# Attention scores as two key tiles with the mask inside the bias, and an order planned with other durations

## The chip, the cores and the metric

The kernel runs on one core of a Trainium2 chip. A core has five engines that run side by side and wait for each other by semaphores: PE (TensorE, the matrix products), DVE (VectorE), ACT (ScalarE), POOL (GpSimd) and SP, which here only issues transfers. PE writes its products to PSUM; DVE and ACT read and write PSUM and SBUF, and POOL works on SBUF. The metric is the device time of one execution in microseconds (us), lower is better.

## The reference

The program is sliding-window attention followed by a mixture of experts, all in float32.

```python
def _attn_ref(q, k, v):                 # q, k, v: (4, 8, 576, 64)
    scores = scale * np.matmul(q, k.transpose(0, 1, 3, 2))
    rel = pos[:, None] - pos[None, :]
    bias = slopes[:, None, None] * (-np.abs(rel).astype(np.float32))[None, :, :]
    mask = (rel >= 0) & (rel < window)  # window = 128
    scores = np.where(mask, scores + bias[None], -1000000000.0)
    scores = scores - np.max(scores, axis=-1, keepdims=True)
    attn = np.exp(scores)
    attn = attn / (np.sum(attn, axis=-1, keepdims=True) + 1e-09)
    return np.matmul(attn, v)

def _moe_ref(x, domain_probs, w1, w2):  # x: (2304, 512), w1: (4, 512, 1024), w2: (4, 1024, 512)
    p = domain_probs / (domain_probs.sum(-1, keepdims=True) + 1e-09)
    for e in range(E):
        h = np.maximum(x @ w1[e], 0.0)
        out += p[:, e:e + 1] * (h @ w2[e])
```

The rows of `x` are the tokens of the attention's output, with the eight heads side by side.

## The kernel before

**The experts.** The 2304 tokens are cut into seven blocks (`BLOCKS`): three of 256 tokens and four of 384. The weights come in 16 units of two tiles of hidden features each, and a pass over the units serves one, two or three blocks, so that 60 loads of both weight matrices are made in all. For one unit and one block, `hidden` makes 24 matmuls (L761) of 256 or 384 columns and `output` makes 6 matmuls of 512 columns for each 128 tokens (L823). A float32 product is made of three: each operand is split into a high part, rounded to the type fp32r that PE takes (`cast`, L278 on ACT, L280 on DVE), and a low part, the difference (`minus`, L288, on DVE or POOL). The products used are high by high, high by low, low by high. Names ending in h and l, such as w1h and w1l, xh and xl, are those parts; rh and rl are the parts of the hidden features (L782 on ACT, L789 on DVE). The output of a unit is weighted and added on DVE (L840).

**The attention.** It works on pairs of heads. A *segment* is one block and one pair of heads; a *unit* is one tile of 128 queries of a segment. There are 18 tiles times 4 pairs, 72 units. The 8 units of the first block are "plain" (PE takes their float32 operands as they are); the other 64 split queries and keys. A query sees at most 128 keys: some of its own tile, the others of the tile before. `pk` is the number of keys of the tile before: 128, or 64 or 0 near the start of a sequence, since sequences of 576 tokens start in a tile's middle. For one unit:

1. scores (L446, plain L437): for each head, queries by `pk + 128` keys, into one PSUM bank `b`.
2. fold: the window has 128 keys, so each query's scores fit in 128 columns of the SBUF tile `s`. A copy (L278 or L280) brings the columns of the tile before; `copy_predicated` on DVE (L482) overwrites with the scores of the query's own tile where a triangular mask says so.
3. `least` (L492, DVE, one for each head): bias plus negated scores, and their minimum. The profile calls it CUSTOM_DVE_ANT_0. It reads `s` and `bias`, both in SBUF; where `pk` is 0 it reads PSUM.
4. `exponents` (L504, ACT, one for each head) with their sums; two small DVE operations on two columns (L520, L529); `weights_`, the division by the sum (L536 on DVE, or L544 twice on ACT).
5. transposes on PE (L569, one for each head, 128 columns), then the high and low part (`hl`; L278/L280, L288).
6. `own` and `others` (L586, L599): POOL's affine_select parts the folded columns again into the keys of the own tile and of the tile before, in `pt`, one of three buffers.
7. values by probabilities (L635) into PSUM `av`, later summed (L658, L661) and split into xh and xl.

**The order.** Nothing is emitted as it is written. Every operation is noted with what it reads and writes, an assumed time for each engine that may take it, and a due time; `Plan.order` simulates the engines greedily, and picks engine, buffer and order from that. Operations are then emitted in the order of their simulated starts, and every engine runs its own queue strictly in that order. The assumed times are the functions `act`, `dve`, `dve2`, `pool`, `mm` at L180 to L185 and constants in `unit`, such as 0.205 us for `least`. DVE and POOL are simulated as independent. Attention of later blocks is spread between the experts' work of earlier ones.

## Time and profile before

| | before |
|---|---|
| median of 3 runs (lowest to highest) | 980.52 us (980.38 to 980.91) |
| span of the profiled execution | 977.4 us |
| median less span | 3.1 us |
| PE busy, matmuls | 925.4 us (95%), 5222 |
| DVE busy | 754.0 us (77%) |
| ACT busy | 352.2 us (36%) |
| POOL busy | 285.6 us (29%) |
| first expert matmul starts | 28.16 us |
| mean granted TensorE clock | 0.995 |

The span runs from the first to the last instruction of one profiled execution. A matmul's recorded duration contains a part in which the next one already streams, so a busy PE may still issue late; the distance between two starts tells what a matmul costs in a stream. For the other engines the busy time includes time in which an instruction has been started and is held up.

### The profile page before, as it was taken

How to read it: one execution, taken by the hardware profiler on the slowest of the kernel's cores; microseconds unless marked ns; L12 is line 12 of the kernel's file. 1: busy time of each engine (PE TensorE's matmuls, PEld its weight loads, DVE VectorE, ACT ScalarE, POOL GpSimd, SP SyncE). 2: the span in 40 equal slices, each digit the busy share in tenths (PEclk: the TensorE clock that was granted, in tenths of full speed). 3: DMA queues.
4: the chain of work that ended last, by engine and by line, in shares of the span. 5: the costliest groups of instructions: out<-in, count | busy, mean ns of one | idle time of the engine just before them, and what ended most of it. 6: DMA issues, size and time to landing. Idle time of an engine off the chain costs nothing.

```text
span 977.4 us, 14432 instructions
## 1 busy us (share of the span) xinstructions
PE 925.4 (95%) x5222; PEld 829.9 (85%) x5222; DVE 754.0 (77%) x1575; ACT 352.2 (36%) x909; POOL 285.6 (29%) x278
## 2 busy tenths in 40 slices
PE   6788898999999999999999999999999999999998
PEld 4677787888888888988888889899999999999997
DVE  5999998898889899888797787866656565656554
ACT  4655445344454555333233432343221212121210
POOL 4667543334434255322232232222101010101000
PEclk9899999999999999999999999999999999999999
DMA  9655433232333345422222211111321121211101
GB/s 235 195 173 171 143 135 114 92 105 84 106 128 117 123 144 191 138 92 83 74 92 82 74 65 58 52 44 65 103 91 66 51 76 46 67 63 65 44 1 65
DMA packets 38359, 95.67 MB, mean 98 GB/s; under 512 B 3728, under 2 KB 15888, under 8 KB 38288
## 3 DMA queue, kind: packets, MB, share of 16 engines
q1 hardware_dynamic: 38288, 94.75, 29.3%
q8 instruction: 41, 0.67, 0.3%
q14 instruction: 30, 0.25, 0.1%
HBM read 90.02 MB, written 4.72 MB: 97 GB/s over the span
## 4 chain that ended last, share of the span: by engine, by line
PE 67%; DVE 26%; issue 3%; DMA 2%; ACT 1%; POOL 1%; DVEq 0%; ACTq 0%; POOLq 0%; SPq 0%
PE b L761 31%; PE b L823 30%; DVE s L492 5%; DVE acc L840 3%; DVE w2l L288 3%; PE av L635 2%; DVE w1l L288 2%; PE b L569 2%; DVE rl L789 2%; DVE qs L288 2%; PE b L446 2%; DVE s L536 1%; DVE s L482 1%; DMA k<-in_qk 1%; DVE x L661 1%
## 5 line engine op out<-in xcount | busy, mean ns | idle before, releaser
L761 PE MATMUL b<-xh,w1h 128*128 128x384 f32 (+1 forms) x896 | 286.8, 320 | 0.0
L761 PE MATMUL b<-xl,w1h 128*128 128x384 f32 (+1 forms) x896 | 281.7, 314 | 0.2 <-DVE xl L288 0.2
L761 PE MATMUL b<-xh,w1l 128*128 128x384 f32 (+1 forms) x896 | 281.7, 314 | 0.0
L840 DVE SCALAR_TENSOR_TENSOR acc<-b,prob,acc 128x512 f32<-128x512 f32 (+1 forms) x271 | 201.7, 745 | 64.9 <-PE b L823 64.2
L782 ACT ACTIVATE rh<-b 128x384 fp32r<-128x384 f32 (+1 forms) x224 | 98.9, 442 | 402.8 <-PE b L761 400.4
L823 PE MATMUL b<-w2l,rh 128*128 128x512 f32 x578 | 227.4, 394 | 0.0
L823 PE MATMUL b<-w2h,rl 128*128 128x512 f32 x578 | 226.9, 393 | 0.0
L823 PE MATMUL b<-w2h,rh 128*128 128x512 f32 x578 | 226.4, 392 | 0.0
L789 DVE SCALAR_TENSOR_TENSOR rl<-b,rh 128x384 fp32r<-128x384 f32 (+1 forms) x224 | 111.0, 495 | 103.8 <-ACT rh L782 102.7
L761 PEld LDWEIGHTS b<-xl,w1h 128*128 128x128 f32 x896 | 170.6, 190 | 5.8 <-DVE xl L288 0.4
L761 PEld LDWEIGHTS b<-xh,w1h 128*128 128x128 f32 x896 | 170.8, 191 | 5.3
L288 POOL TENSOR_TENSOR w1l<-w1r,w1h 128x512 fp32r<-128x512 f32 x60 | 83.6, 1394 | 305.2 <-DVE w1h L280 212.1
L761 PEld LDWEIGHTS b<-xh,w1l 128*128 128x128 f32 x896 | 170.3, 190 | 0.0
L823 PEld LDWEIGHTS b<-w2h,rl 128*128 128x128 f32 x578 | 108.5, 188 | 23.6
L823 PEld LDWEIGHTS b<-w2h,rh 128*128 128x128 f32 x578 | 109.1, 189 | 15.8
L823 PEld LDWEIGHTS b<-w2l,rh 128*128 128x128 f32 x578 | 108.9, 188 | 15.5
L599 POOL TENSOR_SCALAR_AFFINE_SELECT pt<-hl 128x512 fp32r<-128x512 f32 x60 | 42.6, 710 | 235.3 <-DVE hl L288 208.5
L504 ACT ACTIVATE s<-s,t 128x128 f32<-128x128 f32 x128 | 50.8, 398 | 81.8 <-DVE t L492 80.7
L492 DVE CUSTOM_DVE_ANT_0 s<-s,bias 128x128 f32<-128x128 f32 x120 | 75.7, 654 | 1.1
L288 DVE TENSOR_TENSOR w2l<-w2r,w2h 128x512 fp32r<-128x512 f32 x102 | 76.0, 770 | 0.0
L278 ACT ACTIVATE w2h<-w2r 128x512 fp32r<-128x512 f32 x117 | 71.6, 625 | 8.2 <-PE b L823 6.5
L280 DVE CAST w1h<-w1r 128x512 fp32r<-128x512 f32 x92 | 58.8, 653 | 17.5 <-PE b L761 16.2
(89 smaller groups left out, 924.9 us busy)
## 6 DMA issues: line engine op xcount, KB each, us to landing
w1r<-in_w SPq DMA_DIRECT2D x60, 512.0 KB, 3.5
w2r<-in_w SPq DMA_DIRECT2D x60, 512.0 KB, 3.5
q<-in_q SPq DMA_DIRECT2D x16, 384.0 KB, 3.3
k<-in_k SPq DMA_DIRECT2D x12, 512.0 KB, 4.1
k<-in_k SPq DMA_DIRECT2D x12, 384.0 KB, 3.4
out<-acc SPq DMA_DIRECT2D x17, 256.0 KB, 2.0
v<-in_v SPq DMA_DIRECT2D x12, 256.0 KB, 2.7
v<-in_v SPq DMA_DIRECT2D x12, 192.0 KB, 3.0
```

Source lines behind the costliest of these rows:

```text
L278: nc.scalar.activation(o(), i(), AF.Copy)
L280: nc.vector.tensor_copy(o(), i())
L288: by[e].tensor_tensor(out=o(), in0=a(), in1=f(b()), op=ALU.subtract)
L446: nc.tensor.matmul(sc()[:, h, :n], g.qs[:, h, u.q0 : u.q0 + P], m[:, h, u.k0 : u.k0 + n], start=m is g.kh, stop=m is g.kl,)
L492: return lambda e: nc.vector.tensor_tensor_reduce(out=sv()[:, h, :], in0=sv()[:, h, :] if pk else sc()[:, h, :n], in1=(bias if pk else bia ...
L504: return lambda e: nc.scalar.activation(sv()[:, h, :], sv()[:, h, :], AF.Exp, bias=t[:, h : h + 1], scale=-1.0, accum_out=t[:, 2 + h : 3 + h],
L599: nc.gpsimd.affine_select(out=view(dst)[:, :np_, :, o : o + P], in_=f(hl[:, :np_, :, :]), pattern=[[0, 2 * np_], [-1, P]], base=0, channel ...
L761: nc.tensor.matmul(bk[:, :n], a[0][:, kt, fs], b[:, kt, cols], start=kt == 0 and i == 0, stop=kt == KT - 1 and i == 2,)
L782: lambda e: nc.scalar.activation(h[:, :n], bk[:, :n], AF.Relu),
L789: lambda e: nc.vector.scalar_tensor_tensor(out=lo[:, :n], in0=bk[:, :n], scalar=0.0, in1=f(h[:, :n]), op0=ALU.max, op1=ALU.subtract,),
L823: nc.tensor.matmul(bk[:, cs], a[:, ns], b[1][:, fi, cs], start=fi == 0 and j == 0, stop=fi == 1 and j == 2,)
L840: nc.vector.scalar_tensor_tensor(out=o, in0=i_, scalar=p, in1=o, op0=ALU.mult, op1=ALU.add)
```

## The change

The scores are no longer folded. A unit's window is kept as two key tiles, `n = pk + 128` columns for each head. The bias now has 256 columns for each head, and carries the mask: it is loaded twice from the same array (8 transfers in place of 4) and POOL's affine_select writes -1e30 where a key is not seen (8 at the start, in place of 4 and of the mask's own steps). `least` takes the scores straight from PSUM. The copy out of PSUM, `copy_predicated`, the masks, `hl`, `own` and `others` are gone. `exponents` and `weights_` work on up to 256 columns for each head, there are up to four transposes for a unit in place of two, and the high and low parts go straight into one `pt` tile for a whole segment (one buffer in place of three). In the 8 non-plain units whose tile a sequence ends in, POOL copies the pair's bias to a tile and clears a part of it.

The planner gets other durations (PE 0.000452 us a column, POOL 0.00256 us an element, `least` 0.15 + n/960, and so on), a `port` that lets operations on DVE and POOL that take it not overlap in the simulation, and `late`: scores, transposes and values are held ready 1.5 us later than what they wait for.

```diff
@@ Plan.order
-            o.ready = {e: max((d.end + EXTRA + self.GAP[d.eng][e] for d in o.deps), default=0.0) for e in o.engs}
+            o.ready = {e: max((d.end + EXTRA + self.GAP[d.eng][e] for d in o.deps), default=0.0) + o.late for e in o.engs}
...
                     t = max(at[e], o.ready[e], s[0] + 0.2 if s[1] else 0.0)
+                    if e in o.port:
+                        t = max(t, port)
...
                 at[e] = o.end
+                if e in o.port:
+                    port = o.end
@@ durations
-pool = lambda n: 0.1 + n * 0.0022  # noqa: E731
-mm = lambda n: max(n / 2400 + 0.0025, 0.107)  # noqa: E731
+LATE = 1.5
+pool = lambda n: 0.1 + n * 0.00256
+mm = lambda n: max(n * 0.000452, 0.112)
@@ attention_moe
-    places("s", 3, [P, 2, P], F32)
+    places("s", 3, [P, 2, 2 * P], F32)
-    places("hl", 2, [P, 2, 2, P], F32R)
-    places("pt", 3, [P, 2, 2, 256], F32R)
+    pt = sb.tile([P, 2, 2, 2 * QN], F32R, tag="pt", name="pt")
@@ cast, minus
-        plan.op({ACT: act(n), DVE: dve2(n) if sbuf else dve(n)}, emit, due, reads, writes)
+        plan.op(
+            {ACT: act(n), DVE: dve2(n) if sbuf else dve(n)}, emit, due, reads, writes, port=(DVE,) if sbuf else ()
+        )
...
+        engs = {DVE: dve(n), POOL: pool(n)} if gp else {DVE: dve(n)}
+        plan.op(engs, emit, due, reads, writes, port=(DVE, POOL) if gp else ())
@@ unit
+        late = 0.0 if g.plain else LATE
...
-            cast(
-                lambda: sv()[rows, :, P - pk :],
-                lambda: sc()[rows, :, 0:pk],
...
-                lambda e: nc.vector.copy_predicated(
-                    sv(), mask_edge if edge else mask, sc()[:, :, pk:n]
-                ),
...
+        if edge:
+            bb = Buf("x")
+            b2 = lambda: bb[:].rearrange("p (h n) -> p h n", h=2)
+            plan.op(
+                {POOL: 0.75}, lambda e: nc.gpsimd.tensor_copy(b2(), bias[:, hs, :]), d - 1, [*bkey, "scores"], [bb], port=(POOL,)
+            )
...
             return lambda e: nc.vector.tensor_tensor_reduce(
-                out=sv()[:, h, :],
-                in0=sv()[:, h, :] if pk else sc()[:, h, :n],
-                in1=(bias if pk else bias0)[:, 2 * g.hp + h, :],
+                out=sv()[:, h, o:],
+                in0=sc()[:, h, :n],
+                in1=bv()[:, h, o:],
...
-            plan.op({DVE: 0.205}, least(h), d + 0.3, keys, [(s, h), (t, h)])
+            plan.op({DVE: 0.15 + n / 960}, least(h), d + 0.3, [*bkey, bk], [(s, h), (t, h)])
...
-            plan.op({ACT: 0.38}, exponents(h), d + 0.4, [(t, h)], [(s, h), (t, 2 + h)])
+            plan.op({ACT: 0.29 + n * 0.00087}, exponents(h), d + 0.4, [(t, h)], [(s, h), (t, 2 + h)])
...
-        plan.op({DVE: dve(2 * P), ACT: 0.59}, weights_, d + 0.7, [(t, 4)], both)
+        plan.op({DVE: dve(2 * n), ACT: 0.4 + n * 0.00174}, weights_, d + 0.7, [(t, 4)], both, port=(DVE,))
...
             for h in range(2):
-                nc.tensor.transpose(tp()[:, h, :], sv()[:, h, :], ident)
+                for c in (0, P)[2 - w // P :]:
+                    nc.tensor.transpose(tp()[:, h, c : c + P], sv()[:, h, c : c + P], ident)
...
-        def own(e):
-            nc.gpsimd.affine_select(
...
-        def others(e):
-            nc.gpsimd.affine_select(
...
+            part = lambda x: pt[:, x, :, c0 : c0 + w]
+            cast(lambda: part(0), lambda: tp()[:, :, 2 * P - w :], 2 * w, d + 0.9, [bk2], [(g.pt[0], i)], False)
@@ program
+    def seen(part, after):
+
+        return lambda e: nc.gpsimd.affine_select(
+            out=part,
+            in_=part,
+            pattern=[[0, 2], [1, P] if after else [-1, P]],
...
+            compare_op=ALU.is_gt if after else ALU.is_ge,
+            fill=NEG,
+        )
...
+        for i, due in ((1, -37), (0, -33)):
```

What the planner makes of it is seen in the engines' queues. The first place is PE's queue in the stage of the last blocks' attention, for a unit with 192 keys (it is the unit whose scores start at 450.04 us in the profile of before). A row has the line, the operation, what is written from what, and the shape; numbers in names are buffers. In the kernel before:

```order
L446 MATMUL b_125<-kl_72,qs_68 128x192
L761 MATMUL b_129<-xh_92,w1h_100 128x384
...
L823 MATMUL b_126<-w2h_103,rl_114 128x512
L761 MATMUL b_127<-xh_92,w1h_100 128x384
L761 MATMUL b_127<-xl_94,w1h_100 128x384
...
L569 MATMUL b_130<-ident,s_75 128x128 x2
L761 MATMUL b_127<-xh_92,w1h_100 128x384
...
L823 MATMUL b_125<-w2h_103,rh_109 128x512
```

In the changed kernel the same unit stands so (lines L456, L736, L798 and L557 are L446, L761, L823 and L569 of before):

```order
L456 MATMUL b_125<-kl_72,qs_68 128x192
L736 MATMUL b_126<-xh_88,w1h_96 128x384
...
L798 MATMUL b_122<-w2h_99,rl_110 128x512
L736 MATMUL b_123<-xh_88,w1h_96 128x384
...
L736 MATMUL b_123<-xh_88,w1l_98 128x384
L557 MATMUL b_121<-ident,s_75 128x128 x4
L798 MATMUL b_125<-w2h_99,rh_105 128x512
```

Between a unit's scores and its transposes there stood 18 matmuls of 384 columns and 12 of 512; now there are 24 and 12. The transposes moved from the middle of a group of 12 to its end, and there are four of them. Over the 24 units of this stage the matmuls between the two come on average to 5.65 us before and 6.85 us now, at 0.175 us for 384 columns, 0.23 us for 512, 0.12 us for 256 and 0.11 us for 128 (the distances between starts in the timeline), and the least of them to 4.5 us and 5.6 us.

The second place is DVE's queue for the same unit, from just ahead of its fold to the division. ISA is `least` and, on `t`, the reading of its minimum; in the kernel before:

```order
L482 COPY_PREDICATED s_75<-mask,b_125 128x256
L280 CAST qs_68<-q_62 128x768
L492 ISA s_75,t_83<-s_75,bias 128x128
L492 ISA t_83 128x1
...
L288 TENSOR_TENSOR qs_68<-q_62,qs_68 64x768
L789 SCALAR_TENSOR_TENSOR rl_111<-b_129,rh_107 128x384
L520 TENSOR_SCALAR t_83<-t_83 128x2
L840 SCALAR_TENSOR_TENSOR acc_122<-b_128,prob,acc_122 128x512
L529 RECIPROCAL t_83<-t_83 128x2
L536 TENSOR_TENSOR s_75<-s_75,t_83 128x256
```

and in the changed kernel:

```order
L293 TENSOR_TENSOR w1l_97<-w1r_91,w1h_95 128x512
L283 CAST qs_68<-q_62 128x768
L487 ISA s_75,t_83<-b_125,bias 128x192
L487 ISA t_83 128x1
...
L514 TENSOR_SCALAR t_83<-t_83 128x2
L764 SCALAR_TENSOR_TENSOR rl_107<-b_126,rh_103 128x384
L523 RECIPROCAL t_83<-t_83 128x2
L815 SCALAR_TENSOR_TENSOR acc_114<-b_124,prob,acc_114 128x512
```

`least` now reads the bank `b_125`, the low part of the queries no longer stands between it and the sums, and the division has gone to ACT's queue.

The third place is SP's queue near the start, where the operands of the plain units and the first weights are loaded. Before:

```order
L271 DMA dp<-in_dp 128x72
L271 DMA bias<-in_bias 128x256
L271 DMA w1r_95<-in_w 128x1024
L271 DMA q_61<-in_q 128x2x256
L271 DMA k_63<-in_qk 64x1024
L271 DMA w2r_97<-in_w 128x1024
L271 DMA q_62<-in_q 128x2x256
L271 DMA k_64<-in_qk 64x1024
```

and now:

```order
L274 DMA bias<-in_bias 128x2x128 x3
L274 DMA dp<-in_dp 128x72
L274 DMA k_63<-in_qk 64x1024
L274 DMA bias<-in_bias 128x2x128
L274 DMA w1r_91<-in_w 128x1024
L274 DMA bias<-in_bias 128x2x128
L274 DMA q_61<-in_q 128x2x256
L274 DMA k_64<-in_qk 64x1024
```

The third and fourth load of plain operands (`in_qk`) have moved ahead of weights and queries, and four more pieces of bias stand in the queue.

Counted over the whole queues, DVE has 1402 instructions in place of 1577, ACT 818 in place of 767, POOL 194 in place of 283 and PE 5320 in place of 5192. Of the low parts of weights DVE makes 85 + 47 in place of 102 + 60, and POOL 35 + 73 in place of 18 + 60. Of the 64 non-plain divisions ACT makes 48 in place of 22.

More of the change, by code (lines that the diff above doesn't have):

```diff
@@ L11 @@
 F32R = mybir.dt.float32r
-U8 = mybir.dt.uint8
 AF = mybir.ActivationFunctionType
@@ L39 @@
 class Op:
-    __slots__ = ("n", "engs", "emit", "due", "deps", "outs", "wait", "ready", "bufs", "cold", "start", "end", "eng")
+    __slots__ = ("n", "engs", "emit", "due", "deps", "outs", "wait", "ready", "bufs", "cold", "start", "end", "eng", "port", "late")
 class Plan:
@@ L54, in __init__, with op @@
         self.ops, self.last, self.readers, self.places = [], {}, {}, {}
-    def op(self, engs, emit, due, reads=(), writes=(), holds=(), cold=None):
+    def op(self, engs, emit, due, reads=(), writes=(), holds=(), cold=None, port=None, late=0.0):
         o = Op()
@@ L60, in op @@
         o.deps, o.outs, o.bufs, o.start = set(), [], [], None
+        o.port, o.late = (POOL,) if port is None else port, late
         o.cold = 2 * o.engs.get(PE, 0.0) if cold is None else cold
@@ L259, in attention_moe @@
     ident = sb.tile([P, P], F32, tag="ident", name="ident")
[L260 to L263 removed]
+    bias = sb.tile([P, H, 2 * P], F32, tag="bias", name="bias")
     dp = sb.tile([P, NT // P, E], F32, tag="dp", name="dp")
@@ L288, in emit @@
             by[e].tensor_tensor(out=o(), in0=a(), in1=f(b()), op=ALU.subtract)
-        plan.op({DVE: dve(n), POOL: pool(n)} if gp else {DVE: dve(n)}, emit, due, reads, writes)
+        engs = {DVE: dve(n), POOL: pool(n)} if gp else {DVE: dve(n)}
+        plan.op(engs, emit, due, reads, writes, port=(DVE, POOL) if gp else ())
     a, b = EARLY
@@ L426, in unit @@
         n = pk + P
+        o = P - pk
         edge = S - u.tile * P % S
@@ L543, in weights_ @@
             for h in range(2):
-                nc.scalar.activation(sv()[:, h, :], sv()[:, h, :], AF.Copy, scale=t[:, 4 + h : 5 + h])
-        plan.op({DVE: dve(2 * P), ACT: 0.59}, weights_, d + 0.7, [(t, 4)], both)
-        np_ = 1 if g.plain else 2
-        ptag = "acc" if g.plain else "pt"
-        def view(pt):
-            return pt[:].rearrange("p (i h n) -> p i h n", i=1, h=2) if g.plain else pt
-        bk2, u.pt = Buf("b"), Buf(ptag)
-        if pk and u.first:
-            u.pt0 = Buf(ptag)
@@ L567, in transposed @@
+        i = u.q0 // P
+        w = 2 * P if pk else P
+        c0 = 2 * P * i + 2 * P - w
+        if u.first:
+            g.pt = [Buf("acc"), Buf("acc")] if g.plain else ["pt"]
+        bk2 = Buf("b")
+        tp = lambda: bk2[:].rearrange("p (h n) -> p h n", h=2)
         def transposed(e):
             for h in range(2):
-                nc.tensor.transpose(tp()[:, h, :], sv()[:, h, :], ident)
-        plan.op({PE: 2 * mm(P)}, transposed, d + 0.8, [*both, "ident"], [bk2, "transposed"], [hl], 2 * mmc(P))
@@ L572, in unit @@
-        cast(lambda: part(0), tp, 2 * P, d + 0.9, [bk2], [(hl, 0)], False)
-        if not g.plain:
+                for c in (0, P)[2 - w // P :]:
+                    nc.tensor.transpose(tp()[:, h, c : c + P], sv()[:, h, c : c + P], ident)
+        tm = 2 * w // P
+        plan.op(
+            {PE: tm * mm(P)}, transposed, d + 0.8, [*both, "ident"], [bk2, "transposed"], g.pt if g.plain else (), tm * mmc(P), late=late
+        )
+        if g.plain:
+            for h in range(2):
+                cast(
+                    lambda h=h: g.pt[h][:, c0 : c0 + w],
+                    lambda h=h: tp()[:, h, 2 * P - w :],
+                    w,
+                    d + 0.9,
+                    [bk2],
+                    [(g.pt[h], i)],
+                    False,
+                )
+        else:
+            part = lambda x: pt[:, x, :, c0 : c0 + w]
+            cast(lambda: part(0), lambda: tp()[:, :, 2 * P - w :], 2 * w, d + 0.9, [bk2], [(g.pt[0], i)], False)
@@ L637, in values @@
                             v2,
-                            view(pt)[:, i, h, :m],
+                            g.pt[h][:, c : c + m] if g.plain else pt[:, x, h, c : c + m],
                             start=not g.started[h],
@@ L653, in unit @@
                 sum((8 if g.plain else 4) * mmc(j[3]) for j in jobs),
+                late=late,
             )
```

154 lines of the change are left out of this document (47 added, 107 removed).

## The prediction

> **What bounds the kernel now.** I read the page first: the engines' busy time, DVE and the transfers in 40 slices, and the chain of work that ended last.
>
> ```profile
> PE 925.4 (95%) x5222; PEld 829.9 (85%) x5222; DVE 754.0 (77%) x1575; ACT 352.2 (36%) x909; POOL 285.6 (29%) x278
> DVE  5999998898889899888797787866656565656554
> GB/s 235 195 173 171 143 135 114 92 105 84 106 128 117 123 144 191 138 92 83 74 92 82 74 65 58 52 44 65 103 91 66 51 76 46 67 63 65 44 1 65
> PE 67%; DVE 26%; issue 3%; DMA 2%; ACT 1%; POOL 1%; DVEq 0%; ACTq 0%; POOLq 0%; SPq 0%
> ```
>
> PE looks full, yet a quarter of the chain runs through DVE, which is at 90% and more early on. Next come the busy times by stage, cut where the work changes: attention of blocks 1 and 2 beside the first experts, of blocks 3 and 4, of 5 and 6, and experts alone (columns: stretch, length, then PE, PEld, DVE, ACT, POOL busy with instruction counts, granted clock, DMA share, GB/s).
>
> ```profile
> 28.00:175.00 147.00, 128.83 (x814) 112.83 (x815) 140.77 (x313) 78.75 (x218) 80.02 (x76) 0.97 0.47 155
> 175.00:400.00 225.00, 215.18 (x1417) 194.54 (x1417) 202.72 (x471) 106.63 (x292) 93.92 (x85) 1.00 0.37 121
> 400.00:700.00 300.00, 289.37 (x1553) 261.30 (x1552) 232.95 (x480) 103.56 (x266) 78.58 (x80) 1.00 0.22 74
> 700.00:950.00 250.00, 250.00 (x1261) 226.80 (x1260) 148.40 (x226) 48.35 (x90) 19.28 (x15) 1.00 0.18 62
> ```
>
> A PE record overlaps the next, so busy time hides late issue. What a matmul costs in a stream is the distance between starts, in the timeline of PE and, for 256 columns, in the chain:
>
> ```profile
> 440.52 0.39 PE L823 MATMUL b<-w2l,rh 128*128 128x512 f32 x1
> 440.75 0.40 PE L823 MATMUL b<-w2h,rl 128*128 128x512 f32 x1
> 440.98 0.33 PE L761 MATMUL b<-xh,w1h 128*128 128x384 f32 x1
> 441.15 0.34 PE L761 MATMUL b<-xl,w1h 128*128 128x384 f32 x1
> ...
> 442.03 0.38 PE L569 MATMUL b<-ident,s 128*128 128x128 f32 x2
> 442.16 0.42 PE L761 MATMUL b<-xh,w1h 128*128 128x384 f32 x1
> 442.42 0.33 PE L761 MATMUL b<-xl,w1h 128*128 128x384 f32 x1
> ...
> 444.70 0.62 PE L635 MATMUL av<-pt,vs 128*128 128x256 f32 x4
> ```
> ```profile
> 137.32 1.43 PE b L761 x12
> ```
>
> 512 columns take 0.23 us. The six matmuls of 384 columns from 440.98 to 442.03 take 0.175 each, and 12 of 256 in 1.43 are 0.119 each. Two transposes and a 384 take 442.42 - 442.03 = 0.39, so a transpose takes 0.11. Check on the last stage: one unit of weights on 384 tokens is 24 x 0.175 + 18 x 0.23 = 8.34 us for 42 matmuls, and 1261 / 42 x 8.34 = 250 of 250 us: nothing is lost there. With the counts of the two expert lines by stage (L761 first, then L823) I get what PE needs:
>
> ```profile
> 28.00:175.00 147.00, 59.86 (x416) 55.82 (x417) 0.97 0.47 155
> 175.00:400.00 225.00, 105.23 (x761) 98.25 (x760) 1.00 0.37 121
> 400.00:700.00 300.00, 144.63 (x737) 127.14 (x736) 1.00 0.22 74
> ```
> ```profile
> 28.00:175.00 147.00, 49.92 (x192) 33.96 (x192) 0.97 0.47 155
> 175.00:400.00 225.00, 98.05 (x378) 67.34 (x379) 1.00 0.37 121
> 400.00:700.00 300.00, 140.17 (x558) 103.10 (x558) 1.00 0.22 74
> ```
>
> The other matmuls are attention, mostly 128 and 256 wide: 0.115 each. First stage: 416 x 0.119 + 192 x 0.23 + 206 x 0.115 = 117 of 147, 30 lost. Second: 761 x 0.121 (a few are 384 wide) + 378 x 0.23 + 278 x 0.115 = 211 of 225, 14 lost. Third: 737 x 0.175 + 558 x 0.23 + 258 x 0.115 = 287 of 300, 13 lost. So 57 us are lost to late issue. The groups by shape say where:
>
> ```profile
> L569 PE MATMUL b<-ident,s 128*128 128x128 f32 x128 | 27.3, 288 | 34.0 <-DVE s L536 31.5 <-ACT s L544 2.2
> ```
>
> PE stands ahead of transposes for probabilities that DVE finishes late. One such case, in the timelines of DVE, POOL and PE (this unit's scores start at 450.04):
>
> ```profile
> 452.22 2.49 DVE L492 CUSTOM_DVE_ANT_0 s<-s,bias 128x128 f32<-128x128 f32 x1
> ...
> 456.42 0.16 DVE L520 TENSOR_SCALAR t<-t 128x2 f32<-128x2 f32 x1
> ...
> 457.34 0.42 DVE L536 TENSOR_TENSOR s<-s,t 128x256 f32<-128x256 f32 x1
> ```
> ```profile
> 451.97 2.59 POOL L288 TENSOR_TENSOR kl<-k,kh 128x1024 fp32r<-128x1024 f32 x1 [2.48 <-ACT kh L278]
> ```
> ```profile
> 457.91 0.41 PE L569 MATMUL b<-ident,s 128*128 128x128 f32 x2 [1.34 <-DVE s L536]
> ```
>
> `least`, with both operands in SBUF, lasts exactly until POOL's kl ends, and the whole chain slips. The tile view of `s` (minimum, median, maximum in ns) shows that this is a few long ones, and the form that reads PSUM has none:
>
> ```profile
> L492 DVE CUSTOM_DVE_ANT_0 s<-s,bias x120: 272/292/2491, 35.4 to 686.7; 128x128 f32<-128x128 f32 x120
> ...
> L492 DVE CUSTOM_DVE_ANT_0 s<-b,bias x8: 275/280/285, 280.8 to 358.7; 128x128 f32<-128x128 f32 x8
> ```
>
> **The change part by part.** Prices are from these groups (count | busy us, mean ns | idle ahead):
>
> ```profile
> L288 DVE TENSOR_TENSOR w2l<-w2r,w2h 128x512 fp32r<-128x512 f32 x102 | 76.0, 770 | 0.0
> L492 DVE CUSTOM_DVE_ANT_0 s<-s,bias 128x128 f32<-128x128 f32 x120 | 75.7, 654 | 1.1
> L789 DVE SCALAR_TENSOR_TENSOR rl<-b,rh 128x384 fp32r<-128x384 f32 x128 | 70.9, 554 | 95.2 <-ACT rh L782 94.7
> L504 ACT ACTIVATE s<-s,t 128x128 f32<-128x128 f32 x128 | 50.8, 398 | 81.8 <-DVE t L492 80.7
> L789 DVE SCALAR_TENSOR_TENSOR rl<-b,rh 128x256 fp32r<-128x256 f32 x96 | 40.0, 417 | 8.6 <-ACT rh L782 8.0
> L288 DVE TENSOR_TENSOR hl<-b,hl 128x256 fp32r<-128x256 f32 x60 | 25.1, 418 | 1.0
> L482 DVE COPY_PREDICATED s<-mask,b 128x256 f32<-128x256 uint8 x52 | 23.0, 442 | 1.6 <-ACT s L278 0.7
> L536 DVE TENSOR_TENSOR s<-s,t 128x256 f32<-128x256 f32 x42 | 21.7, 516 | 1.2
> ...
> L288 POOL TENSOR_TENSOR w1l<-w1r,w1h 128x512 fp32r<-128x512 f32 x60 | 83.6, 1394 | 305.2 <-DVE w1h L280 212.1 <-PE b L761 56.7 <-ACT w1h L278 26.1
> ```
>
> *PE* gains 120 transposes (248 - 128): 120 x 0.11 = 13.2 us on the path, since PE is the bound wherever it isn't waiting. The plain units' eight lie in the start, where PE waits anyway: nothing.
>
> A rule speaks for more. The Trainium skill, "TensorE: Matmul & The Clock Gate", Part 4: PE-mode transpose, gives about 275 ns for a 128x128 transpose within a kernel, and says it does not keep the clock up. By 0.275 the term would be 33 us and the sum 20 us higher. The trace disagrees: 0.11 from start to start, and the granted clock was 1.00 from 175 us on.
>
> *DVE.* 128 columns more cost 0.137 us (554 - 417). `copy_predicated` goes, 60 x 0.442 = -26.5. `least` from PSUM: 0.280 + 0.137 = 0.417 x 104, with 16 narrower ones at 0.35, is 49 in place of 75.7: -27. Divisions on DVE fall from 42 to 16, now at 0.516 + 0.274 = 0.79: 12.6 in place of 21.7, -9. The probabilities' low part takes 512 columns: 60 x 0.274 = +16. By the order 30 low parts of weights leave DVE: 30 x 0.77 = -23. Sum -70, 754 to 684. The cost of PSUM sources is bounded by the 280 and the 654 rows; I take the first, the same form.
>
> *ACT and POOL.* The exponentials cost some 0.12 more (120 x 0.12 = 14), and 26 divisions of two instructions at 0.398 + 0.12 come over (27); with the wider copies some 45 us are added to 352. POOL loses 120 affine_selects and gains 30 low parts. Both have room as totals; ACT's strict queue is a rival below.
>
> *The order.* The first place in the section on the change shows one group of six matmuls more between scores and transposes, 6 x 0.175 = 1.05 us; over that stage the mean rises from 5.65 to 6.85 and the least from 4.5 to 5.6. In the case above PE waited 1.34. `least` no longer stands still beside kl, which alone was 2.2 us (2.49 - 0.28), so most of these waits should go in stages two and three: of 14 and 13 I leave 4 and 3. What is late next there is the sums' small operations in DVE's queue, held behind rl. In the first stage DVE was busy 140.8 of 147. It loses a quarter of the attention's 47 us (16 of 64 units), 12, and by the order 6 low parts and 5 casts of weights, at up to 0.77 some 7: 122, against PE's 117 + 32 x 0.11 = 121. They are even, so waits stay: I leave 10 of 30, between 4 and all 30.
>
> *New waits.* One `pt` tile serves every segment, where three buffers stood. So the high part of a segment's first unit (ACT or DVE) may not be written before PE has made the last segment's values from the same columns; behind it in ACT's queue stand rh and exponentials, for which PE waits in turn. In the first timeline above values follow the transposes by 2.7 us (442.03, then 444.70), and in the third stage 24 units share 300 us, 12.5 for each, so I cost it at nothing; if each of the 24 segments lost those 2.7 us it would be 65, a bound I hold to be far off. POOL's eight copies of a bias tile (512 elements) must be done before an edge unit's `least`, with which DVE's queue would stand. The trace has no such copy; between nothing and the 1.39 of w1l, also 512 elements, with two inputs, all eight are at most 11 us, on an engine that is busy 29% of the span and has them due a unit ahead. I take nothing, and up to 11 without that lead.
>
> *The start.* Ahead of the third plain load stand 512 KB less (w1r 512 and q 256 gone, two bias pieces of 128 come): at 235 GB/s 2.2 us sooner. Ahead of the fourth it is 256 KB less, 1.1. Four more affine_selects and longer exponentials eat some: -1, between -3 and +3.
>
> Sum: 977.4 - 57 + 17 + 13.2 - 1 = 949.6, plus the 3.1 us by which the median stands above this execution's span: **953 us**.
>
> **The rivals.** (1) *The first stage stays bound by DVE*: low parts of weights (770 ns on average, with their holdups) keep it full and all 30 us stay lost, 20 more than I leave: 973. For it: 122 against 121. Against: the holdups themselves should shrink with 120 fewer SBUF operations. (2) *Transposes at their full length*: 120 x 0.288 = 34.6 in place of 13.2: 974. Against: the 0.39 above; the row's 288 is a duration that overlaps. The page of the Trainium skill that is named above would have this. (3) *ACT takes DVE's place, slower*: 48 of 64 divisions now stand in ACT's queue as two instructions of 0.52, behind exponentials, casts of weights and rh, and the transposes wait for ACT L539 as they did for DVE L536. If that keeps all 57 us lost, the time is 977.4 + 13.2 - 1 + 3.1 = 993. It decides as soon as fewer than 12 of the 57 us are saved. For it: ACT's 78.8 of 147 in the first stage rise by a quarter of the 45, to 90 of some 130. Against: before, PE waited 2.2 us in all for L544 (the row of the transposes above), and ACT is under half busy from 175 us on.
>
> **How the numbers follow.** Forecast 0.66, rival (1) 0.15, (2) 0.04, (3) 0.10, and 0.05 that almost nothing stays lost. Without any lost time the sum is 953 - 17 = 936; the range goes from there to past (1) and (2): 936 to 975. A run can tell about 0.2%, 2 us, from no change. Faster takes all but (3) and the worst of (1): 0.88; within 0.2% 0.03; slower, (3) less a little, 0.09.
>
> **What would show it.** Right: `least` near 0.42 us with no maximum over 1 us; transposes still 0.11 apart; PE idle ahead of transposes down from 34 to under 12 us; experts alone from 700 us on as before, shifted. Wrong: transposes waiting for ACT L539, a first stage (to the 34th rl) still near 147 us long, or DVE busy above 720 us.

## The result and the profile after

The changed kernel takes 940.37 us (median of 4 runs, 939.45 to 943.19), the kernel before, run beside it, 980.71 (median of 4, 980.38 to 982.96). The ratio is 0.9595, with a 95% interval of 0.9575 to 0.9614: 4.1% faster. The forecast was 953, in a range of 936 to 975.

The page of the changed kernel, with the same lines as before: the engines' busy times, DVE in 40 slices, and the chain that ended last.

```profile
PE 928.7 (99%) x5350; PEld 844.8 (90%) x5350; DVE 673.5 (72%) x1400; ACT 403.0 (43%) x960; POOL 244.4 (26%) x189
DVE  4899988887888797767667667656665656556553
PE 96%; DVE 2%; DMA 1%; ACT 1%; issue 0%; POOL 0%; ACTq 0%
```

DVE's share of the chain was 26% and is 2%. The busy times by stage (PE, PEld, DVE, ACT, POOL, then granted clock, DMA share, GB/s), cut where the same amounts of expert work are done:

```profile
28.00:156.00 128.00, 124.24 (x839) 113.84 (x840) 114.56 (x259) 92.96 (x229) 77.80 (x60) 0.99 0.55 179
156.00:400.00 244.00, 244.00 (x1619) 224.76 (x1619) 202.86 (x460) 139.35 (x342) 82.20 (x56) 1.00 0.39 129
400.00:680.00 280.00, 280.00 (x1528) 256.16 (x1527) 192.05 (x393) 108.74 (x251) 61.38 (x46) 1.00 0.22 75
```

From 156 us on PE has no idle time at all. All that it waits for in the whole span stands in six lines, and the group of the transposes has 1.2 us of idle time ahead of it, where it had 34.0:

```profile
PE b L447 <- DMA k<-in_qk: 5.1, 3, 4.3
PE b L736 <- ACT vs L281: 1.9, 1, 1.9
PE b L557 <- DVE s L531: 1.1, 1, 1.1
PE av L609 <- ACT acc L281: 0.5, 1, 0.5
PE b L736 <- DVE xl L293: 0.5, 1, 0.5
PE b L557 <- ACT s L539: 0.2, 1, 0.2
```
```profile
L557 PE MATMUL b<-ident,s 128*128 128x128 f32 x248 | 38.2, 275 | 1.2 <-DVE s L531 1.1 <-ACT s L539 0.2
```

`least` now always reads PSUM, and none is held up. What is held up in its place is the small addition on two columns of `t`, 17 times over 0.6 us, and four of the 16 divisions by the sum on DVE (the tile views of `s` and of `t`; minimum, median, maximum in ns):

```profile
L487 DVE CUSTOM_DVE_ANT_0 s<-b,bias x112: 277/414/425, 31.9 to 649.5; 128x256 f32<-128x256 f32 x88, 128x192 f32<-128x192 f32 x16, 128x128 f32<-128x128 f32 x8
L531 DVE TENSOR_TENSOR s<-s,t x16: 682/692/2086, 70.0 to 587.1; 128x512 f32<-128x512 f32 x14, 128x384 f32<-128x384 f32 x2
```
```profile
L514 DVE TENSOR_SCALAR t<-t x72: 105/169/1755, 6.9 to 650.8; 128x2 f32<-128x2 f32 x72
L523 DVE RECIPROCAL t<-t x72: 145/158/168, 7.2 to 651.0; 128x2 f32<-128x2 f32 x72
```

The longest case, in the timelines of DVE, POOL, ACT and PE. The matmul behind the unit's last score starts at 572.95.

```profile
575.11 1.75 DVE L514 TENSOR_SCALAR t<-t 128x2 f32<-128x2 f32 x1 [0.53 <-ACT s L499]
576.89 0.95 DVE L293 TENSOR_TENSOR qs<-q,qs 64x768 fp32r<-64x768 f32 x1
...
579.01 0.15 DVE L523 RECIPROCAL t<-t 128x2 f32<-128x2 f32 x1
```
```profile
574.17 2.67 POOL L293 TENSOR_TENSOR kl<-k,kh 128x1024 fp32r<-128x1024 f32 x1 [0.95 <-ACT kh L281]
```
```profile
579.26 0.91 ACT L539 ACTIVATE s<-s,t 128x256 f32<-128x256 f32 x2 [3.54 <-DVE t L523]
```
```profile
572.83 0.28 PE L456 MATMUL b<-kl,qs 128*128 128x256 f32 x1
...
581.29 0.60 PE L557 MATMUL b<-ident,s 128*128 128x128 f32 x4
```

This is the same accident as the one quoted in the prediction: DVE stands until POOL's kl ends (574.17 + 2.67 = 576.84, and 575.11 + 1.75 = 576.86; there `least` ended 0.15 us after it), and the chain is 1.6 us late. But the transposes stand 8.3 us behind the scores in PE's queue, with other matmuls between; the division on ACT ends at 580.17, 1.1 us ahead of them, and PE does not wait. The Trainium skill, "SBUF — State Buffer", section "Who interferes with whom", has a rule for it: `tensor_scalar` can take a port pair that DVE shares with GpSimd, and whichever of the two issues first has it for its whole instruction, while the other stands. The trace agrees: all 17 additions that took over 0.6 us start after an operation of POOL has started, and end 22 to 33 ns after it.

To put one number on each stage I add, over all pairs of matmuls that follow each other, the distance of their starts less what that width takes in a full stream (0.109 us for 128 and 192 columns, 0.120 for 256, 0.1745 for 384, 0.231 for 512). That is PE's lost time, waits and low clock together; it is exact to about 1 us. "Start" ends at 28 us, "first" at 175 us in the kernel before and at 160 in all others, "second" at 400, "third" with the attention (700 and 690). All runs of the study are in the table:

| kernel | time | start | first | second | third | last three |
|---|---|---|---|---|---|---|
| before | 980.7 | 17.0 | 29.3 | 13.2 | 13.2 | 55.7 |
| changed | 940.4 | 16.3 | 7.6 | -0.8 | -0.3 | 6.5 |
| e1: LATE = 0 | 958.0 | 14.0 | 16.9 | 3.7 | 2.9 | 23.5 |
| e2: old numbers | 972.7 | 15.8 | 19.0 | 11.4 | 6.1 | 36.5 |
| e3: new planner, old operations | 949.1 | 17.3 | 22.8 | 2.5 | -0.3 | 25.0 |
| e4: transposes twice | 966.9 | 14.1 | 3.2 | -0.6 | -0.2 | 2.4 |
| e5: old numbers, LATE = 1.5 | 952.7 | 15.4 | 14.4 | 2.7 | -0.3 | 16.8 |
| e6: LATE = 2.5 | 953.4 | 14.4 | 16.4 | 2.5 | -0.2 | 18.7 |
| e7: least from SBUF | 960.0 | 14.9 | 18.4 | 4.9 | -0.2 | 23.1 |
| e8: e3, folded in PSUM | 936.1 | 17.2 | 12.2 | 0.7 | -0.4 | 12.5 |
| e9: more on DVE | 945.0 | 13.8 | 11.7 | -0.8 | -0.4 | 10.5 |
| e10: more on ACT | 941.3 | 16.4 | 7.7 | -0.8 | -0.3 | 6.6 |
| e11: LATE = 0.75 | 941.4 | 16.5 | 4.6 | -0.1 | 0.1 | 4.6 |
| e12: e8 in all units | 936.2 | 16.7 | 11.9 | 2.0 | -0.4 | 13.5 |

The same sums of widths say that PE needs 896.9 us before and 910.9 after. So 49.2 us less are lost from 28 us on, 0.7 less at the start, and 14.0 more are needed: 35.9, the difference of the two spans (977.4 and 941.4). The column of the start tells little: e4, e9 and e10 have the changed kernel's order there, and range from 13.8 to 16.4.

### The profile page after: what moved, and what is told of

Read it like the earlier page. It is cut to its first block, busy times and chain, and to the rows that moved or that the text cites. A ratio compares the mean times of both kernels' runs of the same rounds, so it can differ in the third digit from the quotient of the medians.

```text
span 941.4 us, 14382 instructions
## 1 busy us (share of the span) xinstructions
PE 928.7 (99%) x5350; PEld 844.8 (90%) x5350; DVE 673.5 (72%) x1400; ACT 403.0 (43%) x960; POOL 244.4 (26%) x189
## 4 chain that ended last, share of the span: by engine, by line
PE 96%; DVE 2%; DMA 1%; ACT 1%; issue 0%; POOL 0%; ACTq 0%
PE b L736 42%; PE b L798 42%; PE av L609 4%; PE b L557 3%; PE b L456 3%; PE b L447 1%; DMA k<-in_qk 1%; DMA v<-in_v 0%; DVE t L514 0%; DVE xl L293 0%; DVE acc L815 0%; DVE kl L293 0%; DVE w1l L293 0%; ACT s L499 0%; POOL w1l L293 0%
## 5 line engine op out<-in xcount | busy, mean ns | idle before, releaser
L736 PE MATMUL b<-xh,w1h 128*128 128x384 f32 (+1 forms) x896 | 284.6, 318 | 1.9 <-ACT vs L281 1.9
L736 PE MATMUL b<-xl,w1h 128*128 128x384 f32 (+1 forms) x896 | 280.8, 313 | 0.5 <-DVE xl L293 0.5
L736 PE MATMUL b<-xh,w1l 128*128 128x384 f32 (+1 forms) x896 | 281.0, 314 | 0.1
L798 PE MATMUL b<-w2h,rh 128*128 128x512 f32 x578 | 228.2, 395 | 0.0
L798 PE MATMUL b<-w2l,rh 128*128 128x512 f32 x578 | 227.1, 393 | 0.0
L798 PE MATMUL b<-w2h,rl 128*128 128x512 f32 x578 | 227.0, 393 | 0.0
L293 POOL TENSOR_TENSOR w1l<-w1r,w1h 128x512 fp32r<-128x512 f32 x73 | 98.6, 1356 | 479.5 <-DVE w1h L283 218.5
L736 PEld LDWEIGHTS b<-xh,w1h 128*128 128x128 f32 x896 | 169.8, 190 | 7.6 <-ACT vs L281 2.0
L736 PEld LDWEIGHTS b<-xl,w1h 128*128 128x128 f32 x896 | 169.8, 189 | 6.4 <-DVE xl L293 0.7
L736 PEld LDWEIGHTS b<-xh,w1l 128*128 128x128 f32 x896 | 169.5, 189 | 0.3 <-DVE w1l L293 0.3
L798 PEld LDWEIGHTS b<-w2h,rl 128*128 128x128 f32 x578 | 108.5, 188 | 23.6
L798 PEld LDWEIGHTS b<-w2h,rh 128*128 128x128 f32 x578 | 109.0, 189 | 15.8
L798 PEld LDWEIGHTS b<-w2l,rh 128*128 128x128 f32 x578 | 108.8, 188 | 15.8
L499 ACT ACTIVATE s<-s,t 128x256 f32<-128x256 f32 (+2 forms) x128 | 62.6, 490 | 67.4 <-DVE t L487 67.0
L293 POOL TENSOR_TENSOR w2l<-w2r,w2h 128x512 fp32r<-128x512 f32 x35 | 47.9, 1372 | 95.0 <-ACT w2h L281 55.1
L283 DVE CAST w1h<-w1r 128x512 fp32r<-128x512 f32 x85 | 53.8, 642 | 18.1 <-PE b L736 17.9
L293 DVE TENSOR_TENSOR w2l<-w2r,w2h 128x512 fp32r<-128x512 f32 x85 | 61.0, 741 | 0.7 <-ACT w2h L281 0.7
L539 ACT ACTIVATE s<-s,t 128x256 f32<-128x256 f32 (+2 forms) x96 | 42.0, 486 | 29.3 <-DVE t L523 29.0
```

The lines of the kernel that those rows point to most:

```text
L283: nc.vector.tensor_copy(o(), i())
L293: by[e].tensor_tensor(out=o(), in0=a(), in1=f(b()), op=ALU.subtract)
L499: return lambda e: nc.scalar.activation(sv()[:, h, o:], sv()[:, h, o:], AF.Exp, bias=t[:, h : h + 1], scale=-1.0, accum_out=t[:, 2 + h : 3 ...
L539: nc.scalar.activation(sv()[:, h, o:], sv()[:, h, o:], AF.Copy, scale=t[:, 4 + h : 5 + h])
L736: nc.tensor.matmul(bk[:, :n], a[0][:, kt, fs], b[:, kt, cols], start=kt == 0 and i == 0, stop=kt == KT - 1 and i == 2,)
L798: nc.tensor.matmul(bk[:, cs], a[:, ns], b[1][:, fi, cs], start=fi == 0 and j == 0, stop=fi == 1 and j == 2,)
```

## The experiments

Two theories. **A, the order**: the new planner puts more matmul time between a unit's scores and its transposes, and this took PE's waits away. **B, the data path**: fewer operations on DVE, and a `least` that isn't held up beside POOL. The prediction held both: for the second and third stage it named the longer distance first, and then the end of `least`'s holdup as the reason why most waits should go. Ratios are to the kernel before, run on the same chip, with 95% intervals.

**e1**, the order without its allowance:

```diff
-LATE = 1.5
+LATE = 0.0
```

> The changed kernel with LATE = 0.0 in place of 1.5 and nothing else. By the order the mean matmul time between a unit's scores and its transposes falls from 7.6, 7.0 and 6.9 us (blocks 1-2, 3-4, 5-6) to 6.1, 5.5 and 6.0; in the kernel before it was 6.3, 5.9 and 5.7. Theory A (the order took the waits away): PE's idle ahead of transposes comes back from 1 us to over 20, and the time goes from 940 to 965 or more. Theory B (the shorter chain of work on DVE, with least reading PSUM, took them away): that idle stays under 6 us and the time within 6 us of 940. My own guess is between them, about 950.

958.03 us, ratio 0.9768 (0.9748 to 0.9788). PE's idle time ahead of transposes is 9.7 us:

```profile
L557 PE MATMUL b<-ident,s 128*128 128x128 f32 x248 | 40.5, 282 | 9.7 <-ACT s L539 5.0 <-DVE s L531 4.0 <-ACT rh L757 0.6
```

Between the theories: LATE alone is worth 17.7 us, and 22 us of the gain don't need it.

**e2**, the new operations in an order made with the old numbers:

```diff
-LATE = 1.5
+LATE = 0.0
-pool = lambda n: 0.1 + n * 0.00256
-mm = lambda n: max(n * 0.000452, 0.112)
+pool = lambda n: 0.1 + n * 0.0022
+mm = lambda n: max(n / 2400 + 0.0025, 0.107)
...
-                    if e in o.port:
-                        t = max(t, port)
...
-            plan.op({DVE: 0.15 + n / 960}, least(h), ...
+            plan.op({DVE: 0.072 + n / 960}, least(h), ...
...
-            {DVE: 0.19},
+            {DVE: 0.075},
...
```

> The changed kernel's operations, ordered with the planner's numbers of before: LATE = 0, matmul and GpSimd times as before, least and the two small operations on t as short as before, and no shared port in the planner. Mean matmul time between scores and transposes 5.8, 5.7 and 5.5 us, less than before's 6.3, 5.9 and 5.7 with a data path that is itself changed. Theory A (order): most of the 49 us of lost time that went come back, the time is 975 to 990. Theory B (data path): the time stays under 955.

972.65 us, ratio 0.9917 (0.9895 to 0.9939), a little under A's range and far from B's. The tile view of `s`, the waits of PE, and the tile view of `qs` from 400 us on:

```profile
L485 DVE CUSTOM_DVE_ANT_0 s<-b,bias x112: 274/414/428, 32.8 to 679.6; 128x256 f32<-128x256 f32 x88, 128x192 f32<-128x192 f32 x16, 128x128 f32<-128x128 f32 x8
```
```profile
PE b L555 <- DVE s L529: 11.2, 12, 1.5
PE av L607 <- DVE pt L291: 5.8, 8, 1.7
```
```profile
L281 DVE CAST qs<-q x4: 2779/2786/2791, 407.9 to 525.9; 128x768 fp32r<-128x768 f32 x4
```

No `least` is held up here, and the second and third stage still lose 11.4 and 6.1 us of 13.2 each. So freeing `least` wasn't enough. But the waits that are left there still hang on holdups beside POOL, which fall on its neighbours in DVE's queue. All four waits of transposes from 400 us on come 5.9 us after the start of a cast of queries that takes 2.78 us (0.55 in the changed kernel) and stands between `least` and the sums; one case, in the timelines of DVE, POOL and PE:

```profile
407.59 0.35 DVE L485 CUSTOM_DVE_ANT_0 s<-b,bias 128x192 f32<-128x192 f32 x1
407.87 0.08 DVE L485 DVE_READ_ACCUMULATOR2_ANT t<- 128x1 f32 x1
407.87 2.78 DVE L281 CAST qs<-q 128x768 fp32r<-128x768 f32 x1
...
412.15 0.16 DVE L512 TENSOR_SCALAR t<-t 128x2 f32<-128x2 f32 x1
```
```profile
407.84 2.39 POOL L291 TENSOR_TENSOR kl<-k,kh 128x1024 fp32r<-128x1024 f32 x1 [2.52 <-ACT kh L279]
```
```profile
413.77 0.63 PE L555 MATMUL b<-ident,s 128*128 128x128 f32 x4 [1.06 <-DVE s L529]
```

In all four the cast ends 0.42 us after kl. In the second stage the seven such waits come behind a cast or a low part that ends 0.28 to 0.82 us after kl in the same way.

**e3**, the reverse: the kernel before, operations untouched, with LATE, the new times and the shared port in its planner.

```diff
+LATE = 1.5
-pool = lambda n: 0.1 + n * 0.0022
+pool = lambda n: 0.1 + n * 0.00256
-mm = lambda n: max(n / 2400 + 0.0025, 0.107)
+mm = lambda n: max(n * 0.000452, 0.112)
...
+                    if e in o.port:
+                        t = max(t, port)
...
-            plan.op({DVE: 0.205}, least(h), d + 0.3, keys, [(s, h), (t, h)])
+            plan.op({DVE: 0.28}, least(h), d + 0.3, keys, [(s, h), (t, h)], port=(DVE,) if pk else ())
...
```

> The kernel before, with its folded scores, copy_predicated and affine_selects, ordered by the new planner: LATE = 1.5 on scores, transposes and values, the new matmul and GpSimd times, the shared port (least on two SBUF operands counted as using it) and the longer small operations on t. Mean matmul time between scores and transposes 8.3, 8.7 and 8.1 us where it was 6.3, 5.9 and 5.7. Theory A (order): the lost time goes here too, and without the 120 extra transposes the time is 925 to 940, at or below the changed kernel. Theory B (data path): least still stands still beside kl and DVE keeps its 754 us, so half or more of the lost time stays and the time is over 955.

949.11 us, ratio 0.9681 (0.9662 to 0.9700): 31 of the 40 us with every operation as before, though short of A's 940. (The planner chooses engines too: DVE is busy 713.2 us in place of 754.0.) The tile view of `s`, PE's idle time ahead of transposes, and the first two waits that aren't the start's transfers:

```profile
L499 DVE CUSTOM_DVE_ANT_0 s<-s,bias x120: 273/288/2491, 37.4 to 656.0; 128x128 f32<-128x128 f32 x120
```
```profile
L576 PE MATMUL b<-ident,s 128*128 128x128 f32 x128 | 25.4, 279 | 5.2 <-DVE s L543 2.7 <-ACT s L551 2.1 <-ACT rh L790 0.4
```
```profile
PE b L576 <- ACT acc L551: 3.1, 2, 1.5
PE b L453 <- DVE kl L294: 3.1, 1, 3.1
```

In the second stage 17 `least` take over 0.6 us, up to 2.49 (15 in the kernel before), and 2.5 us are lost in place of 13.2: there the order alone is enough, holdups and all. In the third stage only two take over 0.6 us, where 12 did, and none over 0.68, so that stage's -0.3 doesn't show what the distance covers; the new order has moved the holdups away. The first stage keeps 22.8 of 29.3; there the order alone is not enough.

**e4**, the price of a transpose: each of the 248 in the split units is issued twice into the same place, in the same order.

```diff
-                    nc.tensor.transpose(tp()[:, h, c : c + P], sv()[:, h, c : c + P], ident)
+                    for _ in range(1 if g.plain else 2):
+                        nc.tensor.transpose(tp()[:, h, c : c + P], sv()[:, h, c : c + P], ident)
```

> The changed kernel with each of the 240 or so transposes of the split units (248 less none: 248 rows) issued twice into the same place; the planner counts them once, so the order is unchanged. At 0.11 us each, as the prediction took from the distance of starts, 248 more cost 27 us: 967. At the row's duration of 0.275 us (the rival, transposes at their full length) 68 us: 1008. If PE had room beside them, under 950.

966.86 us, ratio 0.9858 (0.9830 to 0.9886). (966.86 - 940.37) / 248 = 0.107 us for one; rival (2) wanted 0.288. The two profiled executions differ by less, 20.9 us or 0.084 each, since 2.2 us less are lost at the start and 4.4 less in the first stage.

**e5**, LATE with all other numbers old; against e2:

```diff
-LATE = 0.0
+LATE = 1.5
```

> The changed kernel's operations with the planner's old numbers and no shared port, as in the run with the old numbers (972.7 us), but with LATE = 1.5. Mean matmul time between scores and transposes 7.7, 7.4 and 6.7 us, as in the changed kernel (7.6, 7.0, 6.9). If the distance alone counts (theory A in its simplest form): 945 or less. If the durations and the port matter beside it, by what they do to the load of DVE (737 us busy with the old numbers, 674 in the changed kernel): 972.7 less the 17.7 that LATE was worth in the first run, 955. If LATE does nothing without them: 970.

952.70 us, ratio 0.9725 (0.9711 to 0.9740), 2 us under the 955 of the second way. With e1, e2 and the changed kernel this makes a table of four: LATE is worth 20.0 us on the old numbers (972.65 - 952.70) and 17.7 on the new, the other numbers 14.6 without LATE and 12.3 with it. The two nearly add. Which of the other numbers does it, the port or a duration, wasn't taken apart. Nor does the mean distance alone set what is lost: in the second stage e1 has 5.5 us between scores and transposes and loses 3.7, e2 has 5.7 and loses 11.4.

**e6**, more of it, in the changed kernel:

```diff
-LATE = 1.5
+LATE = 2.5
```

> The changed kernel with LATE = 2.5 in place of 1.5. Mean matmul time between scores and transposes 8.6, 8.2 and 8.3 us (7.6, 7.0 and 6.9 at 1.5). Theory A: the waits that are left (6 us after the start, nearly all before 150 us) shrink further, 934 to 941. Theory B: no change, 940. Against both: tiles are held longer, and units begin later behind the start; then 942 to 950.

953.43 us, ratio 0.9742 (0.9717 to 0.9767), 13 us slower than at 1.5: the third way, and beyond its 950. The waits of PE from 28 to 160 us:

```profile
PE b L736 <- ACT xh L281: 4.2, 1, 4.2
PE b L798 <- DVE rl L764: 2.6, 2, 1.9
PE b L736 <- DVE xh L283: 2.4, 1, 2.4
```

The wait has changed its place: transposes wait 0.1 us in the whole span, but the first expert matmuls of a block wait for the attention's result xh, which is finished later. POOL also gets less (215.9 us busy against 244.4) and DVE more (693.5 against 673.5), since the planner divides anew.

**e7**, holdups put back into the changed kernel: the split units' scores are copied to SBUF first, and `least` reads the copy.

```diff
+        if not g.plain:
+            cast(lambda: sv()[:, :, o:], lambda: sc()[:, :, :n], 2 * n, d + 0.2, [bk], both, False)
...
-                in0=sc()[:, h, :n],
+                in0=sc()[:, h, :n] if g.plain else sv()[:, h, o:],
```

> The changed kernel, but in the split units the scores are first copied from PSUM to SBUF (on ScalarE or VectorE) and least reads the copy, so that both of its operands lie in SBUF again; LATE stays. By the order the distance becomes 8.4, 7.7 and 7.9 us, since the planner counts the copy. The prediction's mechanism (least stands still beside GpSimd's kl, the chain slips, PE waits): least gets maxima over 1 us again, its mean rises from 415 to 600 ns or more, and over 15 us of PE's waits come back: 955 or more. Theory A: least is held up as well, but the distance takes it in: under 947, of which some us for the copies on a fuller DVE and ACT.

960.02 us, ratio 0.9798 (0.9765 to 0.9831), as B expected.

```profile
L490 DVE CUSTOM_DVE_ANT_0 s<-s,bias x112: 278/420/2606, 30.3 to 665.0; 128x256 f32<-128x256 f32 x88, 128x192 f32<-128x192 f32 x16, 128x128 f32<-128x128 f32 x8
```

By the table 10.8 us of it come back in the first stage, 5.7 in the second and none in the third. It isn't a clean test: the copies lengthen the chain, they put 6 us on DVE beside the holdups (DVE 717.6 us in all, 44 more), and 11 more divisions go to DVE. So it doesn't show that a held-up `least` is what makes PE wait.

**e8**, where e3's first stage goes: e3, but in full units `copy_predicated` writes the own tile's scores over the others in PSUM, and `least` reads PSUM; the first copy and the second SBUF operand go, two transposes a unit stay.

```diff
+        fold = pk == P and not edge
+        if fold:
+            plan.op(
+                {DVE: 0.44},
+                lambda e: nc.vector.copy_predicated(sc()[:, :, :P], mask, sc()[:, :, P:]),
...
+        elif pk:
...
-                in0=sv()[:, h, :] if pk else sc()[:, h, :n],
+                in0=sv()[:, h, :] if pk and not fold else sc()[:, h, : min(n, P)],
...
```

> The kernel before with the new planner (949.1 us as run above), in which the folding of the full units is done in PSUM: copy_predicated writes the own keys' scores over those of the tile before, and least reads PSUM. That drops the first copy of the scores and the second SBUF operand of least, and keeps 2 transposes a unit; units at a sequence's end or with half a tile before them stay as they were. Mean distance 7.9, 6.9 and 6.7 us. PE needs 897 us by the ledger of starts and the start loses 17. If the data path was what kept 25 us of waits in that run: 920 to 932, under the changed kernel. If the first stage is held by something else (GpSimd's affine_selects between transposes and values, low parts): 940 to 949. If copy_predicated on PSUM is slow (over 0.8 us): 950 or more.

936.12 us, ratio 0.9554 (0.9540 to 0.9568): below the changed kernel, by 0.4%, with intervals that don't overlap. In place the operation costs 419 ns, from PSUM to SBUF it took 442:

```profile
PE 913.6 (98%) x5222; PEld 830.2 (89%) x5222; DVE 689.6 (74%) x1478; ACT 373.8 (40%) x963; POOL 304.6 (33%) x300
```
```profile
L479 DVE COPY_PREDICATED b<-mask,b 128x256 f32<-128x256 uint8 x48 | 20.1, 419 | 1.1 <-PE b L444 1.0
```

PE needs 14 us less than in the changed kernel; 6.0 of them are lost again after the start, mostly in the first stage, where 12.2 stay, so the result lies between the 920 to 932 of the first expectation and the 940 to 949 of the second.

**e9 and e10**, the marginal price of DVE and of ACT in the first stage. In the 16 units of blocks 1 and 2 the low part of the probabilities (DVE) is written twice, or the high part (ACT):

```diff
-            by[e].tensor_tensor(out=o(), in0=a(), in1=f(b()), op=ALU.subtract)
+            for _ in range(again):
+                by[e].tensor_tensor(out=o(), in0=a(), in1=f(b()), op=ALU.subtract)
...
+                2 if g.s0 < 768 else 1,
```
```diff
-                nc.scalar.activation(o(), i(), AF.Copy)
+                for _ in range(again):
+                    nc.scalar.activation(o(), i(), AF.Copy)
...
```

> The changed kernel; in the 16 units of blocks 1 and 2 VectorE writes the probabilities' low part twice (the same instruction again, 0.685 us for 512 columns), which the planner doesn't count, so the order is the same. 16 x 0.685 = 11 us more on VectorE, all of it before 160 us. If VectorE's load bounds what is left of the first stage (65 of 72 us busy from 28 to 100 us): 8 to 13 us slower, 948 to 953. If the distance between scores and transposes takes it in: under 943.

> The changed kernel; in the 16 units of blocks 1 and 2 ScalarE writes the probabilities' high part twice (0.596 us for 512 columns) where it does it at all; the order is the same. Up to 16 x 0.6 = 9.6 us more on ScalarE before 160 us (60 of 72 us busy from 28 to 100 us). If ScalarE has room there, as its share says: under 943. If its strict queue bounds the first stage as well (the third rival of the prediction): 946 to 952.

944.99 us, ratio 0.9651 (0.9623 to 0.9679), and 941.29 us, ratio 0.9600 (0.9577 to 0.9623). 11 us more on DVE (684.6 busy in place of 673.5) cost 4.6 by the medians, anything from 2 to 9 by the two intervals; the profiled executions differ by 1.6, with 4.1 more lost in the first stage and 2.5 less at the start. The 13 more on ACT that took place (403.0 to 409.9 us) cost nothing that can be told. So DVE's time has a price in the first stage, and none was seen for ACT's; how large the price is, whether the expected 8 to 13 or half of it, these runs don't tell.

**e11**, between:

```diff
-LATE = 1.5
+LATE = 0.75
```

> The changed kernel with LATE = 0.75. Mean distance 7.2, 6.2 and 6.6 us, between LATE = 0 (6.1, 5.5, 6.0; 958 us) and 1.5 (7.6, 7.0, 6.9; 940 us). On a line between the two: 949. If a threshold near 6 us is enough after 160 us, the later stages lose under 2 us in place of 6.6 and the time is 943 to 947. If the optimum lies lower than 1.5 (2.5 gave 953): under 940.

941.41 us, ratio 0.9592 (0.9571 to 0.9614): the same as at 1.5, and 2 us under the second way. What LATE brings is there at 0.75 already (958, 941, 940), and e6 loses again; whether the best value is 0.75 or 1.5 can't be told.

**e12**, e8's fold for all units:

```diff
-                in0=sv()[:, h, :] if pk else sc()[:, h, :n],
+                in0=sc()[:, h, :P],
...
```

> As the kernel that folds in PSUM (936.1 us), with every unit folded there: in units at a sequence's end and with half a tile before them VectorE clears the columns or rows that aren't seen in PSUM, after the scores (0.28 us), and no least has two SBUF operands any more. Mean distance 7.1, 6.9 and 6.7 us (7.9, 6.9, 6.7). If the held-up least of those units (17.3 us for 32) is part of the 12 us that the first stage still lost: 928 to 934. If it makes no difference, since the half tiles stand mostly later: 935 to 938. If the clearing on VectorE in the chain costs more: 939 or more.

936.15 us, ratio 0.9546 (0.9532 to 0.9561), the second case: no change from e8, though no `least` is held up any more, where 32 took 575 ns. Part of the holdups only moved: the addition on `t` went from 407 to 429 ns on average, 72 times.

## Why the prediction was right

Direction, mechanism in outline and range held; the forecast was 12.6 us too high, and the cause that it gave for two stages was neither enough (e2) nor, in the second, needed (e3).

- **The 57 us to be had** were there: 55.7 by starts. **The 17 us that were to stay were the mis-sized term**: 6.5 stayed. The first stage kept 7.6, near the 10; the second and third, for which 4 and 3 were left, kept nothing (-0.8 and -0.3).
- **Why they went.** "`least` no longer stands still beside kl ..., so most of these waits should go in stages two and three": that step failed. Its premise was sound: in the kernel before each of the 12 waits of transposes from 400 us on comes 4 to 6 us after a held-up `least`. But with `least` freed and an order of the old kind (e2) the holdup falls on other operations of DVE's queue ahead of the sums, and 17.5 of 26.4 us stay lost; 7.1 go in the third stage, 1.8 in the second. And in the second stage of e3 as many `least` are held up as before, and 10.7 of 13.2 go. What covers a chain that is late by a holdup is the order (a mean distance of 7.0 in place of 5.9 us in the second stage, 6.9 in place of 5.7 in the third), as the case at 575 us shows. "What is late next" was to be sums held behind rl; it is the sums' addition held behind POOL.
- **The first stage, "even" at 122 against 121.** The same expert work, to the 34th rl, takes 125 us in place of 145, counted from the first expert matmul (30.4 to 155.8, and 28.2 to 172.9); DVE is busy 114.6 us from 28 to 156. Here both parts are needed: 29.3 us lost before, 19.0 with the operations alone, 22.8 with the planner alone, 7.6 with both. e9 bears out that DVE's time still counts there; e10 finds no price for ACT's.
- **Transposes**: 13.2 forecast, 14.0 by the count (128 more, with the plain units' eight), and 0.107 us each in e4. The 275 ns of the Trainium skill, "TensorE: Matmul & The Clock Gate", Part 4: PE-mode transpose, that were weighed there are the length of the row here too (275 ns). As the price of a transpose between matmuls of a full stream they don't hold, and the granted clock was 1.00 from 156 us on with the transposes in it.
- **DVE** fell to 673.5 us (684 forecast). `least` 415 ns (417 forecast), 344 at 192 columns (0.35), the low part 685 (692), 30 low parts of weights gone: all as priced. Not foreseen were the addition on `t`, 29.0 us in place of 16.3, and low parts of weights that are held up less (741 ns in place of 770, 762 in place of 843). How much of the fall is the operations': 17 us in e2 (736.8); the planner alone makes 41 in e3 (713.2), of which 21 are `least` that is held up less (54.7 us in place of 75.7); in all, 1513 instructions stand on DVE in place of 1575.

```profile
L293 DVE TENSOR_TENSOR w2l<-w2r,w2h 128x512 fp32r<-128x512 f32 x85 | 61.0, 741 | 0.7 <-ACT w2h L281 0.7
L293 DVE TENSOR_TENSOR pt<-b,pt 128x512 fp32r<-128x512 f32 x60 | 41.1, 685 | 9.1 <-ACT pt L281 8.8
L514 DVE TENSOR_SCALAR t<-t 128x2 f32<-128x2 f32 x72 | 29.0, 403 | 17.8 <-ACT s L499 16.6 <-ACT acc L499 0.7
```

- **New waits at nothing**: right. In the tile view of `pt` its writers wait for transposes (PE b L557, 41.6 us) and never for the last segment's values; the `least` behind POOL's bias copies has no idle time ahead of it:

```profile
L487 DVE CUSTOM_DVE_ANT_0 s<-b,x 128x256 f32<-128x256 f32 x16 | 6.2, 415 | 0.0
```

- **The start**: -1 forecast, 17.0 to 16.3 measured, less than executions of one order differ by, so whether it gained can't be told. The order of its loads wasn't tried apart.
- **Median less span**: 3.1 forecast, -1.0 measured (940.37 - 941.4; the profiled execution was the slowest of the four, 943.19). This is 4.1 of the 12.6 us, and it is luck: it hangs on which execution was profiled. The 10.5 of the lost time is the rest, less 0.8 for the transposes, 1.3 for the 55.7 in place of 57 and 0.3 for the start (12.2 in sum; the sum of the forecast was 952.7).
- **The rivals.** (1) fell (7.6 lost, not 30), (2) by e4, (3) since transposes wait 0.2 us for ACT L539 and e10 finds room on ACT.

What stays open: why the last 12 us of e8 and e12 in the first stage are lost, with PE waiting there for several engines in turn, and what the held-up addition on `t` is worth; a kernel without it wasn't tried. Nor was one in which nothing on DVE ahead of the sums is held up, in the old order: e2 frees `least` alone.
